# Four of 64 K loads sent as two transfers of 8 and 120 partitions in a grouped-query attention backward pass

## The chip, the cores and the metric

One core of one Trainium2 chip. The metric is the device time of one execution in microseconds. Before the change three runs gave 671.25, 671.58 and 672.1 us; the median is 671.58.

The engines are called PE (matrix multiplications and transposes), DVE and ACT (elementwise work and evictions from PSUM), POOL (small scalings) and SP, which here issues all transfers. The sixteen units that move data between HBM and SBUF are called DMA engines.

## The reference

Attention of 32 batches with 32 query heads and 4 key/value heads, 4 query positions, 2048 key positions and a head dimension of 128, in bfloat16, and its gradient. Cut to what matters:

```python
def _fwd_reference(q, k, v):                  # q (32,32,4,128); k, v (32,4,2048,128)
    rep = Hq // Hkv                           # 8 query heads share a key/value head
    k = jnp.repeat(k, rep, axis=1)
    v = jnp.repeat(v, rep, axis=1)
    scores = jnp.einsum("bhqd,bhkd->bhqk", q, k) * D ** -0.5
    p = softmax(scores, axis=-1)
    return jnp.einsum("bhqk,bhkd->bhqd", p, v)

def reference(q, k, v, grad_out):
    out, vjp = jax.vjp(_fwd_reference, q, k, v)
    return (out, *vjp(grad_out))              # out, dq, dk, dv
```

K and V are read once and dK and dV written once, 64 MiB each (67.1 MB); the page counts 136.31 MB read from HBM and as much written.

## The kernel before, in words

The host packs each of K and V into two arrays of 32 batches x 128 partitions (the even and odd parts of the keys are interleaved in a row). A row of K has 4224 elements (8448 bytes): 4096 of K and 128 of q in the first array, 128 of grad_out in the second. A row of V has 4096 elements (8192 bytes). dK and dV go out in the same form; the second array of each carries 128 columns of dq or of the output, so it has rows of 8448 bytes.

So every batch has eight transfers of about 1 MB, each of 128 partitions: loads K0, K1, V0, V1 (named LK and LV with part 0 or 1 in the code, line 226) and stores of dV and dK, parts 0 and 1 (SV and SK, line 320). All go out on SP, in one order, into or from 20 slots of [128, 4224] in SBUF (`row`), which loads and results share. Batch 0's loads are cut in two along the row, which makes 260 transfers in all. A transfer is issued when the one eight places before it has landed (eight completion semaphores are used in turn), when its slot is free (a load) or its data is written (a store); one that waits holds up all that stands behind it on SP.

For each batch, PE transposes K and V with fp32 views (line 241), multiplies for scores and for grad_out times V (line 255), for the output and dq (line 288) and for dV and dK (line 310). ACT and DVE evict transposes (lines 207, 209), take the minimum and the exponential (lines 260, 264), form ds (line 303), and evict dV and dK to slots (line 316). POOL scales q and grad_out by the reciprocal sum (lines 271, 274).

The order is written out by hand: `PLAN` is a string with four characters for each step (step, part, place, tile), and `emit` issues the steps in that order under a manual schedule. The steps of one batch are interleaved with those of the batches before and behind it; loads run some batches ahead of their use. The transfers of a batch in the middle stand in this order on SP: K0 of batch b+1, SK1 of b-3, SV1 of b-2, V0 of b, SV0 of b-2, K1 of b+1, SK0 of b-2, V1 of b+1.

Of the kernel before, what the change touches and what calls it, by code (L numbers as in the profile page):

```python
# [14 lines left out]
P = 128  # L15
# [3 lines left out]
BANKS = 8  # L19
SLOTS, E_TILES, DS_TILES = 20, 2, 2  # L20
TILES = dict(KT=8, VT=7, ET=2, DT=2)

NAMES = dict(
    a="LK", b="LV", c="QT", d="QTe", e="KT", f="KTe", g="VT", h="VTe", i="S", j="MX", k="EX", l="RC", m="dop", n="qp",
# [136 lines left out]
def kernel(  # L161
# [11 lines left out]
    nc = tc.nc  # L173
    B, D, C = k0.shape[0], P, 16
    QW = C * P // 4
    Sk = C * P
    k_r, v_r, dk_r, dv_r = (k0, k1), (v0, v1), (dk0, dk1), (dv0, dv1)
# [12 lines left out]
    tiles = {x: [const_pool.tile([P, 8 * P], BF16, name=f"{x.lower()}_sb{i}") for i in range(n)]  # L190
             for x, n in TILES.items()}
    e_sb = [const_pool.tile([P, Sk], BF16, name=f"e_sb{i}") for i in range(E_TILES)]
# [9 lines left out]
    def bank(u, n=1):  # L202
        return psum[:, QW * int(u.where):QW * (int(u.where) + n)]
# [10 lines left out]
    def emit(u):  # L214
        b, name, i = u.b, u.name, u.part
        t = T[b]
        if name in ("LK", "LV"):
            x = slots[int(u.where, 36)]
# [4 lines left out]
            n = LONG if name == "LK" else ROW  # L223
            src = (k_r if name == "LK" else v_r)[i][b]
            for w in (slice(0, Sk), slice(Sk, n)) if b == 0 else (slice(0, n),):
                nc.sync.dma_start(out=x[:, w], in_=src[:, w])  # L226
        elif name == "QT":
            ps = t["qtp"] = bank(u)[:, 0:P]
            for j, x in enumerate(("q", "go")):
# [4 lines left out]
        elif name in ("KT", "VT", "ET", "DT"):  # L234
# [3 lines left out]
            src = t[x, h] if h is not None else t["e" if x == "E" else "ds"][:]  # L238
            src = src.bitcast(FP32).rearrange("p (j d) -> p j d", d=P)
# [4 lines left out]
        elif name in ("S", "DP"):  # L244
# [6 lines left out]
            out = t["S"][:, 2 * QW * i:2 * QW * i + 2 * QW] if name == "S" else t["DP", i]  # L251
            x, side = ("KT", 0) if name == "S" else ("VT", 1)
# [5 lines left out]
        elif name == "MX":  # L258
            t["m"] = sm_pool.tile([P, 1], FP32, name="m")
            nc.vector.tensor_scalar(out=t["e"][:], in0=t["S"], scalar1=-scale, scalar2=None, op0=ALU.mult,  # L260
                                    op1=ALU.min, accum_out=t["m"][:])
        elif name == "EX":
            t["l"] = sm_pool.tile([P, 1], FP32, name="l")
            nc.scalar.activation(out=t["e"][:], in_=t["S"], func=ACT.Exp, bias=t["m"][:], scale=scale,  # L264
                                 accum_out=t["l"][:])
        elif name == "RC":
            t["rinv"] = sm_pool.tile([P, 1], FP32, name="rinv")
            nc.vector.reciprocal(out=t["rinv"][:], in_=t["l"][:])  # L268
        elif name == "dop":
            t["dop"] = sm_pool.tile([P, D], BF16, name="dop_sb", bufs=2)  # L270
            nc.gpsimd.tensor_scalar(out=t["dop"][:], in0=t["go"], scalar1=t["rinv"][:], scalar2=None, op0=ALU.mult)  # L271
        elif name == "qp":
            t["qp"] = sm_pool.tile([P, D], BF16, name="qp_sb", bufs=2)
            nc.gpsimd.tensor_scalar(out=t["qp"][:], in0=t["q"], scalar1=t["rinv"][:], scalar2=scale, op0=ALU.mult,
                                    op1=ALU.mult)
        elif name == "rs":
            t["rs"] = sm_pool.tile([P, 1], FP32, name="rs")
            nc.gpsimd.tensor_scalar(out=t["rs"][:], in0=t["rinv"][:], scalar1=scale, scalar2=None, op0=ALU.mult)
        elif name in ("O", "DQ"):
            if i == 0:  # L280
                t[name] = bank(u)[:, 0:D]
            xt, x = ("ET", "V") if name == "O" else ("DT", "K")
            left = t[xt, i][:].rearrange("p (j q e) -> p j q e", q=P, e=2)
            for c in range(8):
                j, odd = divmod(c, 2)
                for h, r in enumerate(rows):
                    right = t[x, h].rearrange("p (j d e) -> p j d e", d=D, e=2)
                    nc.tensor.matmul(t[name][r, :], lhsT=left[:, j, r, odd], rhs=right[:, 4 * i + j, :, odd],  # L288
                                     start=(i == 0 and c == 0), stop=(i == 1 and c == 7), tile_position=(0, 32 * h))
        elif name in ("Oe", "DQe"):  # L290
            x, by, to = ("o", "rinv", "DV") if name == "Oe" else ("dq", "rs", "DK")
            t[x] = t[to, "out", 1][:, ROW:LONG]
            if u.where == "A":
                nc.scalar.activation(out=t[x], in_=t[name[:-1]], func=ACT.Copy, scale=t[by][:])
            else:
                nc.vector.tensor_scalar(out=t[x], in0=t[name[:-1]], scalar1=t[by][:], scalar2=None, op0=ALU.mult)  # L296
        elif name == "DL":
            t["dl"] = sm_pool.tile([P, 1], FP32, name="delta")
            nc.vector.tensor_tensor_reduce(out=junk[:], in0=t["o"], in1=t["go"], scale=1.0, scalar=0.0,
                                           op0=ALU.mult, op1=ALU.add, accum_out=t["dl"][:])  # L300
        elif name == "DS":
            w = slice(2 * QW * i, 2 * QW * i + 2 * QW)
            nc.vector.scalar_tensor_tensor(out=t["ds"][:, w], in0=t["DP", i], scalar=t["dl"][:], in1=t["e"][:, w],  # L303
                                           op0=ALU.subtract, op1=ALU.mult)
        elif name in ("DV", "DK"):
            i, g = divmod(i, 2)
            acc = t[name, i, g] = bank(u, 2)
            moving, still = ("e", "dop") if name == "DV" else ("ds", "qp")
            for h in (2 * g, 2 * g + 1):
                nc.tensor.matmul(acc[:, QW * (h % 2):QW * (h % 2) + QW], lhsT=t[still][rows[h], :],  # L310
                                 rhs=t[moving][rows[h], QW * i:QW * i + QW], start=True, stop=True,
                                 tile_position=(32 * h, 0))
        elif name in ("DVe", "DKe"):
            i, g = divmod(i, 2)
            copy = nc.scalar.copy if u.where == "A" else nc.vector.tensor_copy
            copy(out=heads_of(t[name[:2], "out", g])[:, :, QW * i:QW * i + QW],  # L316
                 in_=t[name[:2], i, g].rearrange("p (h c) -> p h c", h=2))
        elif name in ("SV", "SK"):
            n = LONG if i else ROW
            nc.sync.dma_start(out=(dv_r if name == "SV" else dk_r)[i][b], in_=t["D" + name[1], "out", i][:, 0:n])  # L320

    with tc.manual_schedule():
        for u in units:
            emit(u)
# [37 lines left out]
```

## Time and profile before

| | value |
|---|---|
| median of three runs | 671.58 us |
| span of the profiled execution | 671.1 us |
| DMA from its first to its last packet record | about 668 us of it |
| PE busy | 607.9 us (91%) |
| DVE busy | 572.0 us (85%) |
| ACT busy | 569.6 us (85%) |
| HBM read and written | 406 GB/s over the span |
| a load or store, issue to landing, median | 18.1 to 20.5 us |
| mean granted TensorE clock | 0.982 |

The span is the time from the first to the last instruction of one execution under the profiler; it is within 0.1% of the median of the runs. A share of busy time is a mean over the whole span. The landing of a transfer is recorded by sixteen events, one for each DMA engine that took part. How far these lie apart tells whether one DMA engine is behind. In the loads of K's second part, with the time of the last event counted from the start of the span:

```
batch   last landing   the 15th before it   the 8th before it   the 1st before it
11        213.3 us           3.55 us              5.95 us             7.87 us
15        297.0              6.26                 8.34               11.86
19        379.0              7.17                 8.94               12.88
23        461.8              8.47                10.18               13.08
30        606.4              6.89                 8.35               12.98
```

The records do not name the DMA engine to which a landing or a packet belongs.

### The profile page before, as it was taken

What the parts mean: (1) busy time and instruction counts of PE and PEld (TensorE: products, weight loads), DVE (VectorE), ACT (ScalarE), POOL (GpSimd) and SP (SyncE); (2) the same over time, 40 slices, a digit from 0 to 9 for tenths busy, and PEclk for the clock granted to TensorE, in tenths of its full rate; (3) what the DMA queues carried; (4) which work ended last, traced back from release to release, by engine and by line L of the source; (5) the groups of instructions that cost most, each with busy time, mean ns of one, the idle gap of its engine ahead of it and who ended that gap; (6) DMA issues with size and microseconds to landing.
All of it is one profiled execution on the core that took longest, in us unless ns stands there. A gap on an engine that the chain in (4) does not pass through costs nothing.

```text
span 671.1 us, 20678 instructions
## 1 busy us (share of the span) xinstructions
PE 607.9 (91%) x8768; PEld 401.4 (60%) x8768; DVE 572.0 (85%) x736; ACT 569.6 (85%) x802; POOL 39.0 (6%) x102
## 2 busy tenths in 40 slices
PE   6998999999998999988998989988999989898993
PEld 5665566666665666655655655655655666565651
DVE  1988799999997999988888989887888979896994
ACT  4997899999997999888888989887888979886894
POOL 0000000000000000000000000000000000000000
PEclk9999999999998999999999999998999989998997
DMA  9999999999999999999999999999999999999867
GB/s 354 417 424 423 419 381 423 423 423 423 423 426 424 424 423 424 424 425 426 414 420 425 413 417 421 414 422 424 396 388 408 417 424 424 404 421 423 347 258 322
DMA packets 37533, 273.97 MB, mean 408 GB/s; under 512 B 4160, under 2 KB 4160, under 8 KB 5184
## 3 DMA queue, kind: packets, MB, share of 16 engines
q1 hardware_dynamic: 37440, 272.65, 98.2%
q8 instruction: 69, 1.13, 0.6%
q14 instruction: 24, 0.20, 0.1%
HBM read 136.31 MB, written 136.31 MB: 406 GB/s over the span
## 4 chain that ended last, share of the span: by engine, by line
DMA 50%; PE 37%; DVE 4%; ACT 4%; issue 3%; SPq 0%; POOL 0%; DVEq 0%; ACTq 0%; POOLq 0%
DMA row<-in_k_dram 50%; PE psum L241 19%; PE psum L310 8%; PE psum L288 5%; PE psum L255 5%; ACT row L316 3%; DVE vt_sb L209 2%; DVE ds_sb L303 1%; DVE row L316 0%; DVE e_sb L260 0%; ACT e_sb L264 0%; PE psum L230 0%; SPq L226 0%; ACT dt_sb L207 0%; DVE row L296 0%
## 5 line engine op out<-in xcount | busy, mean ns | idle before, releaser
L241 PE MATMUL psum<-ident,row 128*128 128x128 f32 x2048 | 290.1, 284 | 28.4 <-DMA row<-in_k_dram 21.5
L316 ACT CAST row<-psum 128x1024 bf16<-128x1024 f32 x292 | 289.2, 1023 | 30.9 <-PE psum L310 29.1
L241 PEld LDWEIGHTS psum<-ident,row 128*128 128x128 f32 x2048 | 224.7, 143 | 94.8 <-issue 32.0
L316 DVE CAST row<-psum 128x1024 bf16<-128x1024 f32 x220 | 264.9, 1217 | 5.7 <-PE psum L310 2.9
L207 ACT COPY kt_sb<-psum 128x512 f32<-128x512 f32 x190 | 110.2, 598 | 20.6 <-PE psum L241 20.4
L207 ACT COPY vt_sb<-psum 128x512 f32<-128x512 f32 x160 | 92.0, 602 | 35.3 <-PE psum L241 34.6
L303 DVE SCALAR_TENSOR_TENSOR ds_sb<-psum,delta,e_sb 128x1024 bf16<-128x1024 f32 x64 | 82.1, 1283 | 13.4 <-PE psum L255 9.0
L310 PE MATMUL psum<-ds_sb,qp_sb 32*128 32x512 bf16 x512 | 76.9, 383 | 3.4 <-ACT row L316 1.0
L260 DVE TENSOR_SCALAR_CACHE_REDUCE e_sb<-psum 128x2048 bf16<-128x2048 f32 x32 | 73.3, 2292 | 5.7 <-PE psum L255 5.7
L310 PE MATMUL psum<-e_sb,dop_sb 32*128 32x512 bf16 x512 | 68.8, 388 | 2.5 <-issue 1.0
L209 DVE COPY kt_sb<-psum 128x1024 bf16<-128x1024 bf16 x66 | 45.0, 685 | 28.4 <-PE psum L241 27.8
L209 DVE COPY vt_sb<-psum 128x1024 bf16<-128x1024 bf16 x96 | 60.7, 684 | 10.0 <-PE psum L241 9.8
L264 ACT ACTIVATE e_sb<-psum,m 128x2048 bf16<-128x2048 f32 x32 | 64.0, 2001 | 0.2 <-DVE e_sb L260 0.2
L271 POOL TENSOR_SCALAR dop_sb<-row,rinv 128x128 bf16<-128x128 bf16 x32 | 19.3, 603 | 605.3 <-DVE rinv L268 530.3
L241 PE MATMUL psum<-ident,ds_sb 128*128 128x128 f32 x256 | 41.8, 286 | 9.6 <-DVE vt_sb L209 7.0
L288 PE MATMUL psum<-row,dt_sb 128*32 128x128 bf16 x2048 | 43.5, 222 | 6.2 <-issue 5.6
L310 PEld LDWEIGHTS <-qp_sb 32*128 32x128 bf16 x512 | 19.4, 91 | 46.1 <-issue 42.6
L255 PE MATMUL psum<-vt_sb,qdt_sb 128*32 128x512 bf16 x512 | 40.7, 388 | 4.6 <-issue 4.5
L288 PEld LDWEIGHTS <-dt_sb 128*32 128x32 bf16 x2048 | 30.8, 95 | 22.0 <-issue 21.1
L241 PEld LDWEIGHTS psum<-ident,ds_sb 128*128 128x128 f32 x256 | 26.9, 140 | 27.2 <-DVE vt_sb L209 16.4
L207 ACT COPY dt_sb<-psum 128x512 f32<-128x512 f32 x63 | 38.4, 611 | 1.0 <-PE psum L241 0.9
L288 PEld LDWEIGHTS <-et_sb 128*32 128x32 bf16 x2048 | 30.4, 95 | 13.8 <-ACT et_sb L207 11.3
(29 smaller groups left out, 310.1 us busy)
## 6 DMA issues: line engine op xcount, KB each, us to landing
out_dram<-row SPq DMA_DIRECT2D x64, 1056.0 KB, 20.1
out_dram<-row SPq DMA_DIRECT2D x64, 1024.0 KB, 20.4
row<-in_k_dram SPq DMA_DIRECT2D x62, 1056.0 KB, 18.1
row<-in_v_dram SPq DMA_DIRECT2D x62, 1024.0 KB, 20.5
row<-in_v_dram SPq DMA_DIRECT2D x4, 512.0 KB, 9.4
row<-in_k_dram SPq DMA_DIRECT2D x2, 544.0 KB, 5.3
row<-in_k_dram SPq DMA_DIRECT2D x2, 512.0 KB, 4.4
```

The lines of the kernel that those rows point to most:

```text
L207: nc.scalar.copy(out=out.bitcast(FP32), in_=in_)
L209: nc.vector.tensor_copy(out=out, in_=in_.bitcast(BF16))
L241: nc.tensor.transpose(out=ps[:, P * j:P * j + P], in_=src[:, 4 * half + j, :], identity=ident32[:])
L255: nc.tensor.matmul(out[r, QW * w:QW * w + QW], lhsT=t["qdt"][:, P * side + 32 * h:P * side + 32 * h + 32], rhs=t[x, NH * i + h][:, QW * w: ...
L260: nc.vector.tensor_scalar(out=t["e"][:], in0=t["S"], scalar1=-scale, scalar2=None, op0=ALU.mult, op1=ALU.min, accum_out=t["m"][:])
L264: nc.scalar.activation(out=t["e"][:], in_=t["S"], func=ACT.Exp, bias=t["m"][:], scale=scale, accum_out=t["l"][:])
L271: nc.gpsimd.tensor_scalar(out=t["dop"][:], in0=t["go"], scalar1=t["rinv"][:], scalar2=None, op0=ALU.mult)
L288: nc.tensor.matmul(t[name][r, :], lhsT=left[:, j, r, odd], rhs=right[:, 4 * i + j, :, odd], start=(i == 0 and c == 0), stop=(i == 1 and c ...
L303: nc.vector.scalar_tensor_tensor(out=t["ds"][:, w], in0=t["DP", i], scalar=t["dl"][:], in1=t["e"][:, w], op0=ALU.subtract, op1=ALU.mult)
L310: nc.tensor.matmul(acc[:, QW * (h % 2):QW * (h % 2) + QW], lhsT=t[still][rows[h], :], rhs=t[moving][rows[h], QW * i:QW * i + QW], start=Tr ...
L316: copy(out=heads_of(t[name[:2], "out", g])[:, :, QW * i:QW * i + QW], in_=t[name[:2], i, g].rearrange("p (h c) -> p h c", h=2))
```

## The change

A table `PARTS` gives, for a step's name, part and batch, the partition ranges in which the transfer goes out. Its default is one range of all 128 partitions. For K's second part in batches 11, 15, 19 and 23 it has two: first partitions 120 to 127, then 0 to 119. Loads and stores both ask the table; no store is in it. SP issues 264 transfers instead of 260; each of the two new ones takes a semaphore of its own in the turn of eight.

```diff
+PARTS = collections.defaultdict(lambda: [slice(0, P)])
+PARTS.update({x: [slice(120, P), slice(0, 120)] for x in {("LK", 1, b) for b in (11, 15, 19, 23)}})
...
             for w in (slice(0, Sk), slice(Sk, n)) if b == 0 else (slice(0, n),):
-                nc.sync.dma_start(out=x[:, w], in_=src[:, w])
+                for r in PARTS[name, i, b]:
+                    nc.sync.dma_start(out=x[r, w], in_=src[r, w])
...
             n = LONG if i else ROW
-            nc.sync.dma_start(out=(dv_r if name == "SV" else dk_r)[i][b], in_=t["D" + name[1], "out", i][:, 0:n])
+            for r in PARTS[name, i, b]:
+                nc.sync.dma_start(out=(dv_r if name == "SV" else dk_r)[i][b][r], in_=t["D" + name[1], "out", i][r, 0:n])
```

## The prediction, made before the result was known

> **What bounds the kernel now.** I read the page's chain of waits, then SP's waits by stretch, then the DMA records, because the chain ends at transfers.
>
> ```profile
> span 671.1 us, 20678 instructions
> q1 hardware_dynamic: 37440, 272.65, 98.2%
> DMA 50%; PE 37%; DVE 4%; ACT 4%; issue 3%; SPq 0%; POOL 0%; DVEq 0%; ACTq 0%; POOLq 0%
> ```
>
> Half of the chain is DMA, and the one data queue keeps 16 DMA engines busy for 98.2% of the span. In order of time the chain reads:
>
> ```profile
> 250.97 1.02 ACT row L316
> 255.24 20.49 DMA row<-in_k_dram
> 585.92 20.43 DMA row<-in_k_dram
> 606.49 1.94 PE psum L241 x16
> 658.91 1.03 ACT row L316
> ```
>
> Up to 255 it steps by compute (the ACT eviction at 212.91, 232.10, 250.97: 19.2 and 18.9 us a batch). From 255 to 606 it is K load after K load, one batch each, 20.4 to 21.2 us; then compute again. SP's waits from 255 to 606 agree:
>
> ```profile
> SPq L320 <- DMA out_dram<-row: 102.8, 51, 2.2
> SPq L226 <- DMA out_dram<-row: 83.7, 17, 5.6
> SPq L226 <- DMA row<-in_v_dram: 69.5, 34, 2.1
> SPq L226 <- DMA row<-in_k_dram: 37.5, 17, 2.8
> ```
>
> 293.5 us of waiting is for transfers to land, not for operands. So the question is what makes a transfer land late. Each transfer has sixteen landing records, one per DMA engine, and one row packet per partition (260 transfers, 260 x 144 = 37440 packets: 128 rows and 16 completions). The last landing stands alone: in the second K load of batch 11 it comes 3.55 us after the fifteenth and 7.9 after the first, in batch 15 6.3 and 11.9, in batch 19 7.2 and 12.9, in batch 23 8.5 and 13.1, in batch 30 6.9 and 13.0. One DMA engine, call it X, is behind all others, and it is nearly always busy. Near the end it works alone; in the window 645.2 to 650.4:
>
> ```profile
> GB/s 0 65 0 65 0 0 65 0 0 65 0 65 0 0 65 0 65 0 65 0 126 65 0 65 0 0 65 0 0 65 0 65 0 0 128 0 65 0 0 65
> q1 hardware_dynamic: 19, 0.14, 6.4%
> ```
>
> 6.4% of sixteen engines is one engine, passing one row after the other. X loses its time in the stores: the distance between its landings, for transfers 130 to 244 in order, has a median of 2.45 us for an 8192-byte-row load and 2.59 for a store, 2.54 and 2.69 with 8448-byte rows. That is 0.14 us more in each of 4 stores a batch, 0.57 us a batch. The other fifteen fall into seven (11 to 13 us ahead of X in batch 30) and eight (6.9 to 8.4 ahead).
>
> **The change part by part.** Four K loads of 128 rows become a transfer of rows 120 to 127 and one of rows 0 to 119, in this order. Bytes and consumers are the same; PE, DVE, ACT and POOL keep their order and their instructions. SP issues 264 transfers in place of 260.
>
> (1) *X's share.* A 128-row transfer gives each engine 8 rows. 120 rows are fifteen such shares, and the eight rows taken off are exactly one: the natural result is that one engine has none of the large transfer, and eight have one row of the small one. If the engine left out is X, it loses 4 x 2.54 = 10.2 us of work, since 2.54 is its landing distance on an 8448-row load. The trace has no transfer of either shape and does not number the engines, so both points are open. The bounds are 10.2 us less for X, and for the case that X gets a row more, 4 x 8448 bytes: four packets of 0.319 us, 1.3 us more. I take the first: partitions 120 to 127 are the last share, and an engine so consistently apart from fifteen others is likely to be at an edge of the row of sixteen.
>
> [...]
>
> (2) *The other fifteen.* Eight of them get one row more each time: 4 x 0.32 = 1.3 us. Whether the large transfer runs at their usual pace is not shown; from below the cost is nothing (same 8 rows), from above that it takes twice as long for some, 2.53 us each, 10.1 in all (15 + 1 rows on eight engines, or two engines in each other's way). I take nothing, as 8 rows an engine is what every row of the trace shows.
>
> (3) *SP and its waits.* Four more issues at 0.34 us each (0.33 to 0.34 in the timeline). SP is waiting for landings at these points, so 1.4 us is hidden; uncovered it would be 1.4. Each transfer waits for the one eight before it. The split takes two of these eight places, so the 120 rows, and the store and V load queued behind them on SP, go out one transfer (2.5 us) later, until the eight have passed. X does not notice: seven transfers stay queued for it. The eight engines of the middle, 2.8 transfers ahead of X, keep four queued. The leading seven, five ahead, may run dry up to 2.5 us per split, 10 in all at most; they have 4.4 us of reserve on the middle group (11.3 less 6.9) at any one time, and regain it. PE waits for K only 14.2 us in the 351 (12 times), and a K load is 20 us under way, so a later issue with an earlier last landing is no new wait.
>
> (4) *Sum.* X would be 10.2 us earlier by the K load of batch 30 (landing at 606.4). There the middle group becomes last: it is 6.9 to 8.4 ahead, and up to 1.3 of that is given back to the extra rows, so the shift is at least 5.6, and 6.9 if the nearest engine gets none. But that group's lead stopped growing after 430 us, when SP waited for X's landings; part of it is held back, and freed. I take 6.5, with 10.2 as the most. Compute can follow: 17 batches at 20.65 us could run at 19.2, 24 us faster. After 606 the chain is compute and only moves with the load. 671.1 - 6.5 = 664.6 in the profiled execution; the median, 671.58, lies 0.5 above that span, so **665.1 us**, 661.0 to 667.5 in its own range (X's full 10.2 us to the smaller bound with 1.5 us given away).
>
> **The rivals.**
>
> *The wrong engine.* X is one of the fifteen. If it is among the eight with the extra row, X is 1.3 us later: 672.9; if it is one of the other seven, nothing changes at the end: 671.6. For it: no record names an engine. Against it: the shares fit one to one. [...] Chance 0.15, of which 0.10 at 671.6.
>
> *The fifteen pay more than they have (slower).* Place: the 120-row transfers on the middle group. Price: up to 8 more row times, 8 x 0.316 = 2.53 us a split, 10.1 in all, against a reserve of 6.9. 671.6 + 10.1 - 6.9 = 674.8. It decides from 1.7 us a split (6.9 / 4). Against it: 26.5 GB/s an engine (8448 bytes in 319 ns) holds with loads and stores mixed. For it: the shape has no precedent here. Chance 0.13. At 0.5 to 1.2 us a split it only eats into the gain: 667.5 to 670, chance 0.10.
>
> *The gain is hidden in compute.* In the first 255 us the chain is compute, and batch 11's split lies there (its load lands at 213). But X is at work through it, so what it saves moves the point where transfers take over. If the saved time of that batch was lost, the other three leave 7.6 us for X, more than the middle group allows: the same 665.
>
> **How the numbers follow.** Forecast 0.62; smaller gain 0.10; wrong engine 0.15; slower 0.13. Below 661 I leave about 0.05 and above 673 about 0.13: range 661 to 673. About 0.2%, 1.3 us, is what a measurement can tell from no change. Faster: 0.62 + 0.10 = 0.72; within: 0.15; slower: 0.13.
>
> **What would show it.** X's lag at the K loads: before 3.55, 6.3, 7.2, 8.5; after the splits it falls by 2.5 to 2.9 each time and the last landing moves into a group of several. Transfers of 120 rows have fifteen landings, those of 8 rows eight. The K load of batch 30 lands near 600 in place of 606.4, the stretch with one busy engine near 645 is gone, and SP's waits for landings from 255 on fall by some 6 us. The forecast is wrong if the last landing stays 7 us alone, or if packets of the 120-row transfers take well over 0.32 us.

## The result, and the profile after

The changed kernel is slower. Four runs gave 678.34 to 680.33 us, median 678.94, against 670.87 to 672.1 (median 671.41) for four runs of the kernel before: a ratio of 1.0107 [1.0093, 1.0121], or 7.5 us. The span of the profiled execution grew from 671.1 to 677.8 us, by 6.7. The forecast was 665.1.

The page of the changed kernel, in the same order as before: span, data queue (packets, MB, share of sixteen DMA engines), shares of the chain, and what was moved in each fortieth of the span:

```profile
span 677.8 us, 20679 instructions
...
GB/s 350 421 424 422 424 403 422 422 424 424 424 425 409 423 423 424 397 401 407 419 418 397 383 401 421 419 384 406 398 424 418 415 420 421 408 408 424 332 266 319
...
q1 hardware_dynamic: 37468, 272.65, 98.1%
...
DMA 55%; PE 33%; ACT 5%; DVE 3%; issue 3%; SPq 0%; POOL 0%; DVEq 0%; ACTq 0%; POOLq 0%
```

The same row of the kernel before:

```profile
GB/s 354 417 424 423 419 381 423 423 423 423 423 426 424 424 423 424 424 425 426 414 420 425 413 417 421 414 422 424 396 388 408 417 424 424 404 421 423 347 258 322
```

The bytes are the same and the queue's share of the span is the same (98.1 against 98.2%), yet the rate fell. A slice is about 17 us. The pieces of 120 partitions land, from their first to their last landing, at 204.8 to 215.3, 286.3 to 300.0, 370.5 to 384.6 and 455.7 to 469.2 us: in the 13th slice, the 17th and 18th, the 22nd and 23rd, the 27th and 28th. There the changed kernel has 409; 397 and 401; 397 and 383; 384 and 406, where the kernel before has 424; 424 and 425; 425 and 413; 422 and 424. So the DMA engines are as busy as before and move less while they are.

The chain of waits in order of time (start, length, what). By compute until 214, then mostly transfers, but now some are stores and V loads:

```profile
213.91 1.25 PE psum L245 x8
215.34 20.55 DMA row<-in_k_dram
...
351.45 19.07 DMA row<-in_k_dram
370.54 19.35 DMA row<-in_v_dram
389.90 20.45 DMA row<-in_v_dram
...
451.44 20.53 DMA out_dram<-row
...
592.58 20.42 DMA row<-in_k_dram
613.13 1.94 PE psum L245 x16
```

The chain leaves transfers at 613.1 instead of 606.5, 6.6 us later, and this shift is the change of the span. SP's waits between 255 and 613 us, as the engine and line that wait, what they wait for, us in total, times, longest:

```profile
SPq L325 <- DMA out_dram<-row: 88.1, 43, 2.4
SPq L230 <- DMA out_dram<-row: 85.4, 23, 5.0
SPq L230 <- DMA row<-in_v_dram: 57.0, 28, 2.3
SPq L230 <- DMA row<-in_k_dram: 46.9, 21, 3.4
SPq L325 <- DMA row<-in_v_dram: 15.6, 6, 3.3
```

The first four sum to 277.4 us over 358 us, against 293.5 over 351 before; with the fifth it is 293.0. SP still does little but wait for landings.

Where the time is lost is best seen in the engine X, the one that lands last. Its landings around batch 19, in us from the start of the span, with the distance to its landing before (worked out from the landing records):

```
transfer          before            after
V1 of batch 18    363.49   2.45     366.68   2.44
K0 of batch 19    366.03   2.54     370.52   3.84
SK1 of batch 15   368.72   2.69     372.86   2.34
SV1 of batch 16   371.43   2.70     375.53   2.67
V0 of batch 18    373.88   2.45     379.29   3.76
SV0 of batch 16   376.47   2.59     381.74   2.46
K1 of batch 19    379.00   2.54     382.05   0.31   (8 partitions)
                                    384.63   2.58   (120 partitions)
SK0 of batch 16   381.61   2.60     387.17   2.53
```

Three things can be read. X is in both pieces: the small one costs it 0.31 us, one row, and the large one a full 2.58. The small piece has eight landings and the large one fifteen. And X loses 1.3 us each (3.84 - 2.54, 3.76 - 2.45) in two loads that were not changed and stand ahead of the split in its queue, while others are already at the 120 partitions. Thirteen of them land their share between 370.5 and 376.2 and one at 380.6: during K0 (from 366.7 to 370.5 us) most of them come to it, and for most of V0 (from 375.5 to 379.3) only the late one is still at it. Its two stores in between lose nothing.

Busy time by stretch there (stretch, length, then PE, PEld, DVE, ACT, POOL busy with their counts, granted clock, share of the sixteen DMA engines, GB/s), changed kernel:

```profile
360.00:368.00 8.00, 6.91 (x170) 4.77 (x172) 6.63 (x11) 7.19 (x11) 1.20 (x3) 1.00 1.00 420
368.00:370.50 2.50, 2.50 (x32) 1.61 (x21) 2.24 (x3) 1.38 (x3) 0.00 (x0) 1.00 0.99 303
370.50:375.50 5.00, 4.96 (x54) 2.77 (x52) 4.78 (x6) 5.00 (x9) 0.00 (x0) 1.00 1.02 393
375.50:379.30 3.80, 2.20 (x18) 1.37 (x14) 2.48 (x3) 3.25 (x6) 0.00 (x0) 1.00 1.00 383
```

Kernel before, at the same transfers:

```profile
354.00:362.00 8.00, 6.88 (x115) 5.12 (x112) 6.95 (x11) 6.96 (x10) 1.20 (x3) 1.00 1.01 426
362.00:369.50 7.50, 6.33 (x120) 3.71 (x112) 5.63 (x10) 5.61 (x9) 0.00 (x0) 1.00 1.01 423
369.50:374.00 4.50, 4.46 (x44) 2.75 (x45) 4.23 (x4) 3.95 (x7) 0.00 (x0) 1.00 1.02 398
```

The DMA share is full in both (0.99 to 1.02), while the rate falls to 303 GB/s in the stretch in which X works on K0: packets take longer. A usual row packet takes 0.309 us (8192 bytes) or 0.319 (8448). Of the row packets that start between 30 and 600 us, 352 of 28482 last over 0.48 us before and 570 of 28204 after. The median of these is 0.68 us before and 0.64 after, about twice the usual time. So a few packets are slowed much, and not all a little. To which engine or transfer a slow packet belongs, the records do not say.

### The profile page after: what moved, and what is told of

The parts are those of the page before. It is cut to its first block, busy times and chain, and to the rows that moved or that the text cites. A ratio compares the mean times of both kernels' runs of the same rounds, so it can differ in the third digit from the quotient of the medians.

```text
span 677.8 us, 20679 instructions
## 1 busy us (share of the span) xinstructions
PE 607.7 (90%) x8768; PEld 401.5 (59%) x8768; DVE 572.1 (84%) x736; ACT 569.7 (84%) x802; POOL 39.0 (6%) x102
## 3 DMA queue, kind: packets, MB, share of 16 engines
q1 hardware_dynamic: 37468, 272.65, 98.1%
## 4 chain that ended last, share of the span: by engine, by line
DMA 55%; PE 33%; ACT 5%; DVE 3%; issue 3%; SPq 0%; POOL 0%; DVEq 0%; ACTq 0%; POOLq 0%
DMA row<-in_k_dram 31%; PE psum L245 17%; DMA out_dram<-row 12%; DMA row<-in_v_dram 12%; PE psum L314 7%; PE psum L292 4%; PE psum L259 4%; ACT row L320 4%; DVE vt_sb L212 2%; DVE ds_sb L307 1%; DVE row L320 0%; ACT e_sb L268 0%; DVE e_sb L264 0%; PE psum L234 0%; ACT kt_sb L210 0%
```

## The experiments

Each is the changed kernel with the table `PARTS` altered as shown. Ratios are to the kernel before on the same chip. The table after the last experiment gives X's shift along each run. In the expectations, Theory A is that partitions handed to other DMA engines slow the packets, and Theory B that the number of transfers costs the time. The shared way into SBUF that the expectations name for Theory A is the author's supposition: the records give a packet's time and size, not its way.

**Number of transfers, without touching partitions.** The same four loads go out in two transfers of all 128 partitions, cut along the row at column 2048.

```diff
-PARTS.update({x: [slice(120, P), slice(0, 120)] for x in {("LK", 1, b) for b in (11, 15, 19, 23)}})
+            halves = name == "LK" and i == 1 and b in (11, 15, 19, 23)
-            for w in (slice(0, Sk), slice(Sk, n)) if b == 0 else (slice(0, n),):
+            for w in (slice(0, Sk), slice(Sk, n)) if b == 0 or halves else (slice(0, n),):
```

> The same four K loads go out as two transfers of all 128 partitions, the row cut in two (4096 and 4352 bytes). Eight places in the turn of eight and the issues are as in the changed kernel; every DMA engine keeps its rows and its partitions. Theory A (partitions handed to other DMA engines make two of them share a way into SBUF, packets of 0.32 us take 0.5 to 0.65, and the late engine X pays whenever it is loading): within 1.3 us of before, 671.4 +- 1.3. Theory B (X pays 0.32 us for the extra row, and the rest, some 5 us, comes from transfers issued later because the split takes two of eight places): 675 to 678.

Measured: 671.04 us (10 runs) against 671.94 (13), 0.9986 [0.9976, 0.9995]. Busy time by stretch at batch 19:

```profile
363.00:375.00 12.00, 11.52 (x149) 7.35 (x138) 10.47 (x12) 10.32 (x16) 0.00 (x0) 1.00 1.01 422
```

The rate stays at 422 GB/s, and X takes 1.24 and 1.35 us for the two pieces, 2.59 together against 2.54 whole. Four more issues and four more places in the turn of eight cost nothing. The 0.9 us of gain does not show at the first three cuts: from batch 11 to 20 X is within 0.1 us of where it stood ahead of the first one.

**The other end of the partitions.** Partitions 0 to 7 and 8 to 127.

```diff
+PARTS.update({x: [slice(0, 8), slice(8, P)] for x in {("LK", 1, b) for b in (11, 15, 19, 23)}})
```

> Partitions 0 to 7 and 8 to 127 in place of 120 to 127 and 0 to 119. The counts of DMA engines, rows and places are as in the changed kernel. Theory A: slower than before by 3 to 8 us (674 to 680), again with packets near 0.6 us while the large piece runs; X's hits of 1.25 us may fall on other transfers, because other partitions are written by strangers. Theory B: as the changed kernel, 678 to 680.

Measured: 678.89 us (4 runs), 1.0095 [1.0067, 1.0123], as with partitions 120 to 127. X is in both pieces again. So taking the rows off at the other end does not leave X out either.

**Halves.** Partitions 0 to 63 and 64 to 127: sixteen landings each, nobody gets a row more, nobody is left out.

```diff
+PARTS.update({x: [slice(0, 64), slice(64, P)] for x in {("LK", 1, b) for b in (11, 15, 19, 23)}})
```

> Partitions 0 to 63 and 64 to 127: 16 DMA engines with 4 rows each in both pieces, so X has no extra row and no DMA engine is left out. [...] Theory B: as with the cut along the row, 675 to 678, and packets of 0.32 us.

Measured: 681.71 us (4 runs), 1.0126 [1.0094, 1.0158], at least as slow as the two cuts of 8 and 120 (the intervals overlap). Busy time by stretch at batch 19:

```profile
360.00:366.00 6.00, 4.86 (x42) 3.75 (x41) 5.04 (x9) 5.34 (x9) 1.20 (x3) 1.00 1.01 426
366.00:372.00 6.00, 5.11 (x156) 3.08 (x154) 4.41 (x9) 4.29 (x5) 0.00 (x0) 1.00 1.03 379
372.00:376.00 4.00, 4.00 (x43) 2.57 (x40) 3.86 (x5) 3.68 (x6) 0.00 (x0) 1.00 1.01 352
376.00:382.60 6.60, 4.77 (x45) 2.75 (x44) 5.03 (x5) 6.05 (x10) 0.00 (x0) 1.00 1.01 319
```

426 GB/s falls to 379, 352 and 319 at a full DMA share. X takes 1.25 us for its share of the first half, the pace of four rows, and 2.54 for the second, twice that. So it is in batch 15 too (1.25 and 2.58); in batch 11 both halves are slow (2.63 and 2.12) and in batch 23 neither (1.27 and 1.26). Neither an extra row nor an uneven share is there to blame, so a cut across partitions has a price of its own.

Four of X's eight halves took 2.12 to 2.63 us and the other four 1.25 to 1.27. Why some take twice as long, and whether on the side of SBUF or of HBM, no run here separates.

**Which engine is X?** Each of the four loads goes out as partitions 0 to 111 and two pieces of 7 and 9, 6 and 10, 5 and 11, 4 and 12. The author assumes that the engines get the rows of a small piece in a fixed order, one row each; then the smallest piece that X is in gives its place in that order, which the expectations count from 0.

```diff
+PARTS.update({("LK", 1, b): [slice(0, 112), slice(112, 112 + n), slice(112 + n, P)]
+              for b, n in ((11, 7), (15, 6), (19, 5), (23, 4))})
```

> Three pieces each: partitions 0 to 111, then 16 more in pieces of 7 and 9 (batch 11), 6 and 10 (15), 5 and 11 (19), 4 and 12 (23). If n rows use the n lowest DMA engines with one row each, the landing of a small piece is alone 4 to 7 us late exactly when X is among these n. This gives X's number: in 8 of 8 and not in 7 of 7 means number 7. Theory A expects slow packets (0.5 us and more) around all small pieces; the time is not what is asked, some 675 to 690.

Measured: 683.12 us (2 runs), 1.0161 [1.0128, 1.0194]. The last landing of the piece of 7 rows lies 6.3 us behind the others, of 6 rows 8.1, of 5 rows 13.0. With 4 rows all four land within 1.5 us, 11.6 us before X lands its share of the 112. The pieces of 9, 10, 11 and 12 rows all have X. So X is in the pieces of 5 rows and more and not in that of 4. This fits the assumed order, with X in the fifth place, number 4 in the expectations from here on; the order itself is not shown, as the records do not number the engines.

**One split.** Only batch 19.

```diff
+PARTS.update({("LK", 1, 19): [slice(120, P), slice(0, 120)]})
```

> Only the split of batch 19 is left, as 120 to 127 and 0 to 119. If each split costs X its extra row (0.32 us) and one or two hits of about 1.25 us by strangers on its way into SBUF, the time is 672 to 674.5, a quarter of the whole loss give or take one hit, and X's landings move at that place alone. If the loss comes from the number of transfers or a general drift, it would be spread over the span.

Measured: 674.48 us (5 runs) against 672.17 (12), 1.0035 [1.0023, 1.0048], 2.3 us. X takes 1.48 us more in K0 of batch 19, 0.76 more in V0 of batch 18 and 0.31 in the small piece. Busy time by stretch:

```profile
350.00:362.00 12.00, 10.53 (x150) 7.42 (x149) 10.58 (x14) 10.20 (x16) 1.20 (x3) 1.00 1.02 427
364.50:377.00 12.50, 11.13 (x125) 7.25 (x113) 9.95 (x11) 10.54 (x16) 0.00 (x0) 1.00 1.00 339
377.00:390.00 13.00, 10.91 (x205) 7.32 (x203) 10.79 (x17) 9.15 (x15) 1.20 (x3) 1.00 1.01 424
```

427 before, 339 in the 12.5 us in which the large piece is written for the most part, 424 after. Of the row packets over 0.48 us, 137 lie between 350 and 390 us; the kernel before has 24 there. In this execution X's shift shrinks again, from 2.1 us at batch 20 to 1.2 at batch 30, and its last store, far from the split, takes 1.4 us longer than before; so the 2.6 us by which this span (673.7) is longer are not all the split's.

**The same cut in stores.** The second dK store of batches 8, 12, 16 and 20 as 120 to 127 and 0 to 119; all loads whole.

```diff
+PARTS.update({x: [slice(120, P), slice(0, 120)] for x in {("SK", 1, b) for b in (8, 12, 16, 20)}})
```

> The loads are whole again; the second dK store of batches 8, 12, 16 and 20 goes out as partitions 120 to 127 and 0 to 119. X (number 4) gets the extra row in each, 4 x 0.334 = 1.3 us. Theory A1 (the shared way is that of writes into SBUF): 672 to 673.5, no cluster of packets near 0.6 us at these stores. Theory A2 (any change of partitions between DMA engines slows both directions): 676 to 680, with such clusters.

Measured: 676.24 us (4 runs), 1.006 [1.0044, 1.0077], 4.1 us, as Theory A2 had it. Busy time by stretch at batch 12, whose split store lands between 296.8 and 310.0 us:

```profile
290.00:300.00 10.00, 7.88 (x70) 5.35 (x69) 7.76 (x10) 8.03 (x12) 1.20 (x3) 1.00 1.01 419
300.00:310.00 10.00, 9.61 (x200) 6.05 (x198) 9.14 (x14) 8.64 (x13) 0.00 (x0) 1.00 1.00 368
310.00:322.00 12.00, 9.31 (x81) 6.55 (x80) 9.20 (x11) 9.23 (x15) 1.20 (x3) 1.00 1.02 429
```

A split store slows rows too, at about half of the price of a split load (4.1 against 7.5 us for four): 42 row packets over 0.48 us start between 300 and 320 us, where the kernel before has 2. Whether the slowed rows are the store's own or those of loads beside it, the records do not say. In the split stores themselves X loses hardly more than the extra row (0.23 to 0.39 us). Between batches 8 and 24 no single loss of X is above 0.81 us; three of the four over 0.45 are in K or V loads, one is in a whole store.

**Relief of X without taking it out of a load.** SK1 of every second batch from 8 to 22 goes out as partitions 0 to 111 and four pieces of four partitions, which go to the first four engines if the order assumed above holds, so that X has seven rows instead of eight.

```diff
+PARTS.update({x: [slice(0, 112)] + [slice(r, r + 4) for r in range(112, P, 4)]
+              for x in {("SK", 1, b) for b in range(8, 24, 2)}})
```

> The second dK store of batches 8, 10, ... 22 (eight stores) goes out as partitions 0 to 111 (7 rows for every DMA engine) and four pieces of 4 partitions, which numbers 0 to 3 take. X gives away one row in each, 8 x 0.334 = 2.7 us; numbers 0 to 3 get three more, 8.0 us in all. If X alone sets the time and reads from SBUF are not slowed (A1), the time falls to 668.5 to 670. With A2 it rises to 674 or more. If X is not what sets the time, it stays at 671.4.

Measured: 675.52 us (6 runs, 672.47 to 677.46), 1.0055 [1.0039, 1.0071]. In the profiled execution, the lowest of the six (span 670.7), the last landing of all is 0.4 us earlier than before, but at the second K load of batch 30 the next engine is only 0.9 us ahead of the last instead of 6.9: it lands 6.2 us later than it did. X was relieved, and others came level with it. Part of this was to be expected: 8.0 us of extra rows for four engines (an estimate, 24 rows of 0.334 us) is more than the lead of 6.9. From batch 16 on, the last piece of four lands behind the last share of the 112 (389.59 against 388.98 us there, 432.06 against 430.80 in batch 18), so the engine that lands last is then at times one of these four and not X. So the run does not show what a relief of X alone would give. Why the other five executions were 1.5 to 5 us slower than the profiled one is not recorded. None of the cuts across partitions gave a kernel faster than the one before.

**The same cut at a place where X is loading.** V0 of batches 10, 14, 18 and 22 instead of K1. The faster engines are three to five transfers ahead of X (7 to 13 us in batch 19 before the change, at about 2.6 us a transfer). Three and four places ahead of K1 on SP stand two stores, SV1 and SK1; three and four places ahead of V0 stand two loads, K0 and V1.

```diff
+PARTS.update({x: [slice(120, P), slice(0, 120)] for x in {("LV", 0, b) for b in (10, 14, 18, 22)}})
```

> The same split, 120 to 127 and 0 to 119, but of V's first part in batches 10, 14, 18, 22, two places earlier on SP than the K loads of the change. DMA engines 7 to 13 us ahead of X run it while X is three to five transfers behind, which here is mostly at K0 and V1 (loads), where for the K loads of the change it is mostly at SK1 and SV1 (stores). If X is slowed by strangers writing its partitions only while it writes too, each split now costs the extra row (0.31 us) and 2 to 3.5 us of hits on K0 and V1: 681 to 686. If it does not matter what X is doing, the loss is that of the change, 678 to 680.

Measured: 685.87 us (4 runs) against 672.08 (7), 1.0206 [1.018, 1.0231], 13.8 us, with the same bytes and the same number of pieces. All large losses of X are in loads: K0 of batch 11 1.26 us; V1 of batch 14 1.22, K0 of batch 15 0.73 and V0 of batch 14 2.17; V1 and V0 of batch 18 1.65 and 1.74; V1 and V0 of batch 22 0.96 and 1.82. So the price of a split depends on its place. The time came out as expected, but in part by luck: the hits on K0 and V1 are there, at 0.96 to 1.95 us a split instead of 2 to 3.5, but three of the four splits also lose 1.7 to 2.2 us in the cut V0 itself (0.3 of it the extra row). In the change the cut K1 itself cost 1.20 us in batch 11, 0.31 in 15 and 0.35 in 19. Why X is slowed in a cut V0 and hardly in a cut K1 stays open, and the run also changed the array and the length of the rows.

X's landing (the last of each transfer) after minus before, in us, in the profiled executions:

```
                 K0 of 11   K1 of 12   K1 of 16   K1 of 20   K1 of 24   K1 of 30   last store
the change         -0.3        1.5        3.1        5.7        7.2        6.6        6.9
along the row      -0.3       -0.2       -0.2       -0.3       -0.6       -1.2       -1.6
0 to 7             -0.3        3.7        3.7        4.9        6.2        5.6        6.8
halves              1.4        3.9        5.8        9.6       11.0       10.5       10.3
7+9 ... 4+12       -0.9        2.5        4.1        8.7       11.9       11.5       11.3
only batch 19       0.0       -0.2       -0.3        2.1        1.8        1.2        2.7
stores SK1          0.5        1.3        2.8        4.6        4.4        4.6        4.5
SK1, 112+4x4       -0.7       -0.1       -0.4        0.9        1.7        0.2       -0.4
V0 (10 ... 22)      1.5        1.3        5.7        9.5       12.4       12.1       12.1
```

The large steps come at the splits. Between them, ahead of the first and at the very end, the rows scatter by up to 1.5 us (the 1.4 of the halves lie ahead of their first split). K0 of 11 stands ahead of the first split on SP in every row; in the V0 row it stands only three places ahead, and X loses 1.26 us in it. In the row "SK1, 112+4x4" the last landing behind batch 16 is not always X's.

## Why the prediction was wrong

*What bounds the kernel* was read rightly. X's shift at batch 30, 6.6 us, and at its last store, 6.9, is the change of the span, 6.7; the stretch near the end in which X works nearly alone is still there, between 651.8 and 657 us (packets, MB, share of sixteen engines; one engine would be 6.3%):

```profile
q1 hardware_dynamic: 38, 0.21, 9.9%
```

*Step (1), "If the engine left out is X, it loses 4 x 2.54 = 10.2 us of work",* failed first, at the choice between the two bounds. The landings show X in both pieces, among the fifteen with the 120 rows and the eight with a row more: 4 x 0.31 to 0.32 = 1.3 us more instead of 10.2 less. The reason given, that an engine apart from fifteen others is likely to be at an edge, was no reading of the profile; the profile could not name X, and the step made a forecast of a guess. The rival "the wrong engine" had this mechanism and this price (672.9), but it accounts for 1.3 of the 6.7 us.

*Step (2), "I take nothing, as 8 rows an engine is what every row of the trace shows",* is the step that cost most. Every transfer of the trace also had all 128 partitions, and this is what the cut changes. The rest, 6.7 - 1.3 = 5.4 us, or 1.35 a split, X loses in transfers around the splits (1.3 us each in K0 of batch 19 and V0 of batch 18), where row packets over 0.48 us gather (81 start between 280 and 300 us, 3 before the change); that these long packets are X's is inferred, as packets do not name their engine. Its upper bound, "twice as long for some, 2.53 us each", would have held; the working charged it to the fifteen alone, which have a reserve of 6.9 us, and not to X, which has none. So did the slower rival (674.8, decides from 1.7 us a split): longer packets were right in kind, but X pays from the first microsecond. Step (4) took its 6.5 us from these two steps and fell with them.

What slows the rows is not shown. The runs show no loss in a cut along the row (0.9986), loss with no uneven share in the halves (1.0126), loss with cut loads (1.0107) and with cut stores (1.006), and X losing in loads more than in stores (1.3 us in each of two loads ahead of the split of batch 19, nothing in the two stores between them). That rows of two transfers hinder each other would fit all of this, but it is the author's reading: no record names the partition or the place of a packet, and a cause on the side of SBUF was not told apart from one on the side of HBM.

*Step (3)* was right: the four extra issues and places cost nothing (0.9986 along the row).

*The signs to look for.* Eight and fifteen landings came as said. X's lag over the fifteenth rose in batch 11 (5.6 us instead of 3.6), but then fell, as a success would have shown it: 4.0 us instead of 7.2 in batch 19, 3.2 instead of 8.5 in batch 23, 5.3 instead of 6.9 in batch 30. But at batch 30 X came 6.6 us later and the fifteenth 8.2 us later: the lag shrank because the others fell back. The sign that decided was the other one named, packets of well over 0.32 us.

*The rival "hidden in compute"* could not be tested, as there was no gain.

*The number of transfers* is not what costs: two halves, with sixteen landings in each, had a price, 1.0126, and the cut along the row, with as many transfers, had none, 0.9986.

## What to carry to other kernels

Where a large transfer must be cut on a busy queue, cut it along the row and keep all 128 partitions; here that was free (0.9986), and every cut across partitions was slower (1.0035 to 1.0206). Before work is taken off a DMA engine that lags, find out which it is, with small pieces of falling size, and look at when it lands and not at how far it lags. A full DMA share is no full rate (339 GB/s at a share of 1.00 in the run with one split, 424 behind it at 1.01): read the GB/s beside it, stretch by stretch.

## What the hardware showed that was not expected

One DMA engine of the sixteen, X, is slower in stores than in loads: 2.59 us against 2.45 for 1 MB, 2.69 against 2.54 with the longer rows. Of all row packets of 8192 bytes, loads and stores together, 13333 of 14256 take exactly 0.309 us (30 to 600 us), so most other engines have no such difference. Why, whether by the engine or by the partitions of its rows, stays open.

Around a transfer that is cut across partitions, load or store, some row packets of 8 KB take about 0.6 us instead of 0.31 (137 against 24 between 350 and 390 us with one cut load), while the DMA share stays full (1.00 from 364.5 to 377 us there); the same 8 + 120 cut in four loads cost 7.5 us on K1 and 13.8 us on V0.
